# A threshold attention with a SwiGLU block: weight steps, x.T copies, key tails and q transposes moved between engines

## Chip, cores and metric

The kernel runs on one core of a Trainium2 chip. The metric is the device time of one execution in microseconds (us), the median of several runs. The profile is one execution recorded by the hardware profiler; its span is a little shorter than the device time.

## What is computed

Attention with a threshold for 8 batches, 8 heads, 576 positions and head size 64, and behind it a SwiGLU block over the 4608 tokens (model width 512, hidden width 1536). All is float32.

```python
scores = scale * np.matmul(q, k.transpose(0, 1, 3, 2))
thresh = np.max(scores, axis=-1, keepdims=True) - tau
scores = np.where(scores >= thresh, scores, -1000000000.0)
attn = np.exp(scores - np.max(scores, axis=-1, keepdims=True))
attn = attn / (np.sum(attn, axis=-1, keepdims=True) + 1e-09)
x = np.matmul(attn, v)              # (B,H,S,D) -> (B*S, H*D)
g = x @ w_gate
out = (g * (1.0 / (1.0 + np.exp(-g))) * (x @ w_val)) @ w_out
```

The weights come as float64 and are turned into float32 on the chip.

## The kernel before

**Order of work.** The schedule is written out by hand: each engine executes its instructions in the order in which the program issues them. The main loop goes over 36 segments. A segment is a pair of heads of one batch (`i`, 32 pairs, four to a batch) with a list of query tiles. The first four segments do tiles 0 and 1 of the first batch's pairs; the next four (segments 4 to 7, in the order of pairs 3, 0, 1, 2) do tiles 2, 3 and 4 of the same pairs; from segment 8 on a segment is a whole pair of a later batch with five tiles. A tile has 128 queries, and tile 4, the *short* tile, has the last 64. `TA = 2` tells the early tiles of the first batch from the late ones, `NT = 4` is the number of the short tile.

**One tile.** `scores` multiplies q and k on TensorE (PE; score banks `sc`), VectorE (DVE) takes the maximum (L328 in the first batch, L318 and L274 later), ScalarE (ACT) makes the threshold `th` (L333, later L330) and the exponential (L334), and VectorE masks and sums in one instruction (L338), which frees the score banks. The reciprocal `ri` follows; the normalisation (L352, L354) is shared between GpSimd (POOL) and ScalarE.

**First batch.** The probabilities have queries on the partitions. `flip` transposes them on PE one tile later: four blocks of 128 keys per head (`tp`, L396, or L398 where the normalisation is folded into the unit matrix, as in the early tiles), and the last 64 keys of each head by a product with the identity into the tile `end` (L400). ScalarE copies both to SBUF (L401, L406), and `attend_tile` multiplies with v (L421, L425); ScalarE copies the result into x.T (L427).

**Later batches.** The scores are laid out so that VectorE's own transposes of 32x32 blocks do the turning (L376). `attend` multiplies a whole pair with v (L447) in the second tile of the following pair, into two PSUM tiles `xa`, and then copies them into x.T: four copies of 128x128 (L458) and four of 64x32 (L466), alternately on VectorE and on ScalarE.

**q and k.** `prepare` transposes a pair's q and k on VectorE, one tile before the pair begins. In the first batch it does k (L758), the queries of the early tiles (L759), and the rest of q into a place of its own (L764; for pair 0 L763, one pair later).

**Weights.** 24 pieces pass through three steps, one piece further per tile: `fetch_weights` loads a piece (L182, L179), `split_weights` takes its high and low words apart on ScalarE (L193, L194), and `join_weights` puts them together: three instructions on VectorE (L202, L204, L205) and one on GpSimd (L207). In the main loop a tile's split stands ahead of its second half and its join behind the masking. What is not joined in time is done by `need`, ahead of the first product that uses it.

**SwiGLU.** Between the steps of a tile, `fill` issues gate and value products (`pg`, `pv`, L486) and output products (`po`, L554, L587), as many as `pace` allows. ScalarE takes the gate out of PSUM (`tn` L499, `gt` L500), VectorE multiplies with the value (L506), and GpSimd finishes the product (L518).

PSUM has two score tiles (`ps_s`, two banks each) and four banks for everything else (`ps_f`).

Of the kernel before, what the change touches and what calls it, by code (L numbers as in the profile page):

```python
# [19 lines left out]
def kernel(  # L20
# [30 lines left out]
    nc = tc.nc  # L51
# [224 lines left out]
    def same(out, in_):  # L276
        nc.scalar.copy(out, in_[:, :, 0])  # L277

    def scores(seg, t):
        qT, kT, tiles, halved = seg["qT"], seg["kT"], seg["tiles"], seg["halved"]  # L280
        if halved and "p" not in seg:
            seg["p"] = arenas[seg["i"] % 2]
        q0 = t * P - seg["q0"]
        heads = [slice(h * D, (h + 1) * D) for h in range(2)]
        if t < NT:
            pss = [ps_s.tile([P, 2, 512], F32, name="sc") for _ in range(2)]
            at = [t, NT + 1 + t]
        else:
            pss = [ps_s.tile([P, 2, 512], F32, name="sc")]
            at = [t]  # L290
        if halved:
            put = [(pss[u], h, q0 + u * D) for u in range(len(pss)) for h in range(2)]
            for x in range(0, len(put), 2):
                for g in range(NG):
                    a, c = divmod(g, 2)
                    for ps, h, col in put[x:x + 2]:
                        hs = heads[h]
                        nc.tensor.matmul(ps[g * G:(g + 1) * G, h, 0:SH], qT[hs, col + a * G:col + (a + 1) * G],  # L298
                                         kT[hs, c * SH:(c + 1) * SH], start=True, stop=True)
        elif t < NT:  # L300
            for h, hs in enumerate(heads):
                for n in range(2):
                    nc.tensor.matmul(pss[h][:, n, 0:SH], qT[hs, q0:q0 + P], kT[hs, n * SH:(n + 1) * SH],
                                     start=True, stop=True)
        else:
            for n, h in ((0, 0), (1, 1), (1, 0), (0, 1)):
                hs = heads[h]
                nc.tensor.matmul(pss[0][hs, n, 0:SH], qT[hs, q0:q0 + D], kT[hs, n * SH:(n + 1) * SH],
                                 start=True, stop=True)
        mx, nm, th, ri = (stp.tile([P, 4, 2] if x == "mx" else [P, 4], F32, name=x) for x in ("mx", "nm", "th", "ri"))  # L310
        sm = sums[0]
        sums.rotate(1)
        if halved:
            m = 2 * len(at)
            scs = [ps[:, h, 0:SH] for ps in pss for h in range(2)]
            ps = [seg["p"][:, x, u * SH:(u + 1) * SH] for u in range(2) for x in at]
            for x, tile_ in enumerate(pss):
                nc.vector.tensor_reduce(out=mx[:, 2 * x:2 * x + 2, 0], in_=tile_[:, :, 0:SH], axis=AX.X, op=ALU.max,  # L318
                                        negate=True)
            meet(mx, m, largest)  # L320
            nc.vector.tensor_reduce(out=nm[:, 0:m], in_=mx[:, 0:m, :], axis=AX.X, op=ALU.min)  # L321
        else:
            m = len(at)
            scs = [ps[:, :, 0:SH] for ps in pss]
            ps = [pbufs[0][:, x, :].rearrange("p (n s) -> p n s", n=2) for x in range(m)]
            pbufs.rotate(1)
            for x in range(m):
                nc.vector.tensor_reduce(out=nm[:, x:x + 1], in_=scs[x], axis=AX.XY, op=ALU.max, negate=True)  # L328
        if halved:
            nc.scalar.activation(th[:, 0:m], nm[:, 0:m], AF.Identity, bias=cut, scale=-1.0)  # L330
        for x in range(m):
            if not halved:
                nc.scalar.activation(th[:, x:x + 1], nm[:, x:x + 1], AF.Identity, bias=cut, scale=-1.0)  # L333
            nc.scalar.activation(ps[x], scs[x], AF.Exp, bias=nm[:, x:x + 1])  # L334
        yield
        turn(1)
        for x in range(m):
            nc.vector.scalar_tensor_tensor(out=ps[x], in0=scs[x], scalar=th[:, x:x + 1], in1=ps[x],  # L338
                                           op0=ALU.is_ge, op1=ALU.mult, accum_out=sm[:, x, 0:1])
        tot = stp.tile([P, 4], F32, name="tot")  # L340
        if halved:
            yield
            meet(sm, m, same)
            yield
            nc.vector.tensor_reduce(out=tot[:, 0:m], in_=sm[:, 0:m, :], axis=AX.X, op=ALU.add)
        else:
            nc.vector.tensor_reduce(out=tot[:, 0:m], in_=sm[:, 0:m, 0:3:2], axis=AX.X, op=ALU.add)
        nc.vector.reciprocal(out=ri[:, 0:m], in_=tot[:, 0:m])  # L348
        if t >= TA or halved:
            for x in range(m):  # L350
                if x % 2:
                    nc.gpsimd.tensor_scalar(out=ps[x], in0=ps[x], scalar1=ri[:, x:x + 1], scalar2=None, op0=ALU.mult)  # L352
                else:
                    nc.scalar.activation(ps[x], ps[x], AF.Copy, scale=ri[:, x:x + 1])  # L354
        if not halved:
            yield
        if halved:
            unturned.append([seg["p"][:, x, :] for x in at])
        else:
            units = [ident] * m  # L360
            if t < TA:

                units = [dbufs[0][:, x, :] for x in range(m)]
                dbufs.rotate(1)
                for x in range(m):
                    nc.scalar.activation(units[x], ident, AF.Copy, scale=ri[:, x:x + 1])
            unflipped.append((seg, t, [(p.rearrange("p n s -> p (n s)"), unit) for p, unit in zip(ps, units)]))
            yield
        yield

# [10 lines left out]
    def flip():  # L381

        if not unflipped:
            return
        seg, t, ps = unflipped.popleft()
        n = P if t < NT else D
        pT = pTbufs[0][:, 0:2 * KT * n].rearrange("p (h t q) -> p h t q", h=2, t=KT)
        pT2 = pTbufs[0][:, 2 * KT * n:(2 * KT + 1) * n]
        pTbufs.rotate(1)
        end = ps_f.tile([P, 512], F32, name="end", tag="psf")  # L390
        for h, (p, unit) in enumerate(ps):
            tp = ps_f.tile([P, 512], F32, name="tp", tag="psf")
            for kt in range(KT):
                ks = slice(kt * P, (kt + 1) * P)
                if unit is ident:
                    nc.tensor.transpose(tp[:, ks], p[:, ks], unit)  # L396
                else:
                    nc.tensor.matmul(tp[:, ks], p[:, ks], unit, start=True, stop=True)  # L398
            if t < NT:
                nc.tensor.matmul(end[h * D:(h + 1) * D, 0:P], p[:, KM:S], unit, start=True, stop=True)  # L400
                nc.scalar.copy(pT[:, h], tp.rearrange("p (t q) -> p t q", q=P))  # L401
            else:
                for hs in (slice(0, D), slice(D, P)):
                    nc.tensor.matmul(end[hs, 0:D], p[hs, KM:S], unit[hs, hs], start=True, stop=True)
                nc.scalar.copy(pT, tp.rearrange("p (t h q) -> p h t q", h=2, q=D))
        nc.scalar.copy(pT2, end[:, 0:n])  # L406
        unattended.append((seg, t, pT, pT2))
# [21 lines left out]
    def attend(seg):  # L429
# [21 lines left out]


        per = TC // (2 * G)
        puts = deque([nc.vector.tensor_copy, nc.scalar.copy])
        for a in range(R):
            for u in range(NU):
                i0 = 1 + u * per
                puts[0](xts["full", b * NU + u][:, cc, :, a, :],  # L458
                        xa[a][:, i0 * G:(i0 + per) * G].rearrange("d (i q) -> d i q", q=G))
                puts.rotate(1)  # L460
        at = b % BT
        for h in range(2):
            hs = slice(h * D, (h + 1) * D)
            cs = slice((1 + m) * G, (2 + m) * G) if h == 0 else slice(0, G)
            for a in range(2):
                puts[0](xts["last", b // BT][hs, cc, at, a], xa[a][hs, cs])  # L466
                puts.rotate(1)
        yield


# [267 lines left out]

    raws = {}
    kept = {}  # L740

    def fetch_qk(i):
        if i < NPAIR and i not in raws and i not in kept:
# [2 lines left out]
    def prepare(seg):  # L746
# [8 lines left out]
        if i < NP:  # L755
# [1 line left out]
            rest = flat[:, i * (S - QA):(i + 1) * (S - QA)]  # L757
            nc.vector.transpose(out=kT, in_=kr)  # L758
            nc.vector.transpose(out=qT[:, 0:QA], in_=qr[:, 0:QA])  # L759
            if i:  # L760
                if i == 1:

                    nc.vector.transpose(out=flat[:, 0:S - QA], in_=raws[0][0][:, QA:S])  # L763
                nc.vector.transpose(out=rest, in_=qr[:, QA:S])  # L764
            kept[i] = {"kT": kT, "qT": rest, "q0": QA}
        else:
            kT = qkp.tile([P, S], F32, name="kT")
# [17 lines left out]
    for n, seg in enumerate(segs):  # L785
        if NP <= n < 2 * NP:
            seg["v"] = segs[seg["i"]]["v"]
        for x, t in enumerate(seg["tiles"]):
# [28 lines left out]
            fill(part)  # L817
            next(go)
            gates()
            if attends and n > 2 * NP:  # L820
                next(products)
                next(products)
# [50 lines left out]
```

## Time and profile before

| | |
|---|---|
| time, median of 3 runs | 1536.05 us (1534.77 to 1539.76) |
| span of the profiled execution | 1532.6 us |
| PE busy | 1487.4 us (97%) |
| DVE busy | 1024.3 us (67%) |
| ACT busy | 729.7 us (48%) |
| POOL busy | 644.4 us (42%) |

Busy time of PE is modelled from pipelined matmuls, so a busy PE need not be at its peak. A mean share over the whole span mixes stages with different limits; the stages are read one by one below. Names such as `sc`, `pall` or `wgv` are tiles of the program, L338 is line 338 of the kernel, and an arrow in brackets names what ended an engine's wait.

### The profile page before, as it was taken

How to read it: one execution, taken by the hardware profiler on the slowest of the kernel's cores; microseconds unless marked ns; L12 is line 12 of the kernel's file. 1: busy time of each engine (PE TensorE's matmuls, PEld its weight loads, DVE VectorE, ACT ScalarE, POOL GpSimd, SP SyncE). 2: the span in 40 equal slices, each digit the busy share in tenths (PEclk: the TensorE clock that was granted, in tenths of full speed). 3: DMA queues.
4: the chain of work that ended last, by engine and by line, in shares of the span. 5: the costliest groups of instructions: out<-in, count | busy, mean ns of one | idle time of the engine just before them, and what ended most of it. 6: DMA issues, size and time to landing. Idle time of an engine off the chain costs nothing.

```text
span 1532.6 us, 31424 instructions
## 1 busy us (share of the span) xinstructions
PE 1487.4 (97%) x11792; PEld 1126.1 (73%) x11792; DVE 1024.3 (67%) x3150; ACT 729.7 (48%) x2045; POOL 644.4 (42%) x646
## 2 busy tenths in 40 slices
PE   6999889899999999999999999999999999999998
PEld 5766564477777777787777777777777777888887
DVE  6867988777777677756777777767776776522212
ACT  5777755555455545443454545544544454311110
POOL 3444544348354444435443545443535354400011
PEclk9999999999999999999999999999999999999999
DMA  8533312211111111110111111211101120000000
GB/s 199 137 104 125 87 30 53 50 39 32 27 29 41 29 32 46 46 32 14 36 29 46 32 46 32 46 32 41 26 27 31 46 47 15 1 14 1 14 15 14
DMA packets 176488, 66.93 MB, mean 44 GB/s; under 512 B 159696, under 2 KB 159696, under 8 KB 176336
## 3 DMA queue, kind: packets, MB, share of 16 engines
q1 hardware_dynamic: 168656, 54.88, 15.9%
q0 software_dynamic: 2944, 9.44, 1.7%
q8 instruction: 94, 1.54, 0.4%
q10 hardware_dynamic: 4736, 0.59, 0.3%
q14 instruction: 58, 0.48, 0.1%
HBM read 55.44 MB, written 9.44 MB: 42 GB/s over the span
## 4 chain that ended last, share of the span: by engine, by line
PE 85%; DVE 9%; ACT 2%; issue 1%; DMA 1%; SPq 1%; POOLq 0%; POOL 0%; DVEq 0%; ACTq 0%
PE pv L486 24%; PE pg L486 23%; PE po L587 19%; PE xa L447 8%; PE sc L298 8%; DVE pall L338 2%; DVE mx L318 2%; DVE pall L376 1%; DVE mx L274 1%; ACT pall L334 1%; DMA vall<-in_v_dram 1%; PE tp L396 1%; ACT sums L277 1%; SPq L242 0%; PE xa L421 0%
## 5 line engine op out<-in xcount | busy, mean ns | idle before, releaser
L352 POOL TENSOR_SCALAR pall<-pall,ri 128x288 f32<-128x288 f32 (+1 forms) x260 | 265.2, 1030 | 427.3 <-DVE ri L348 376.0
L486 PE MATMUL pg<-xall,wgv 128*128 128x256 f32 x1728 | 401.5, 384 | 1.3 <-ACT xall L427 1.3
L486 PE MATMUL pv<-xall,wgv 128*128 128x256 f32 x1728 | 401.6, 383 | 0.0
L486 PEld LDWEIGHTS pg<-xall,wgv 128*128 128x128 f32 x1728 | 324.4, 190 | 68.1 <-issue 17.9
L486 PEld LDWEIGHTS pv<-xall,wgv 128*128 128x128 f32 x1728 | 325.5, 191 | 64.4 <-issue 20.0
L338 DVE SCALAR_TENSOR_TENSOR pall<-sc,th,pall 128x288 f32<-128x288 f32 (+1 forms) x540 | 258.0, 528 | 24.3 <-ACT pall L334 24.3
L334 ACT ACTIVATE pall<-sc,nm 128x288 f32<-128x288 f32 (+1 forms) x540 | 236.3, 510 | 0.5
L318 DVE TENSOR_REDUCE mx<-sc 128x2 f32<-128x576 f32 x252 | 177.8, 742 | 31.3 <-PE sc L298 30.4
L354 ACT ACTIVATE pall<-pall,ri 128x288 f32<-128x288 f32 (+1 forms) x264 | 132.0, 540 | 104.8 <-DVE ri L348 103.5
L376 DVE STREAM_TRANSPOSE pall<-pall 128x576 f32<-128x576 f32 x252 | 181.3, 754 | 0.2 <-POOL pall L352 0.2
L298 PE MATMUL sc<-kT,qT 64*32 64x288 f32 x4032 | 158.6, 413 | 21.7 <-DVE pall L338 20.7
L587 PE MATMUL po<-wo,ht 128*128 128x256 f32 x768 | 176.2, 382 | 0.0
L506 DVE SCALAR_TENSOR_TENSOR ht<-tn,pv 128x512 f32<-128x512 f32 x102 | 69.8, 685 | 149.9 <-PE pv L486 147.1
L277 ACT COPY sums<-sums 32x4 f32<-32x4 f32 (+1 forms) x560 | 108.4, 194 | 124.0 <-DVE pall L338 112.7
L587 PEld LDWEIGHTS po<-wo,ht 128*128 128x128 f32 x768 | 144.4, 190 | 27.7 <-issue 4.6
L330 ACT ACTIVATE th<-nm,cut 128x4 f32<-128x4 f32 (+1 forms) x140 | 41.6, 297 | 231.8 <-DVE nm L321 231.8
L499 ACT ACTIVATE tn<-pg 128x512 f32<-128x512 f32 x108 | 64.9, 601 | 152.7 <-PE pg L486 152.0
L298 PEld LDWEIGHTS sc<-kT,qT 64*32 64x32 f32 x4032 | 59.1, 106 | 99.1 <-issue 71.4
L447 PE MATMUL xa<-pall,vall 64*64 64x288 f32 x2016 | 128.9, 405 | 0.6 <-issue 0.6
L518 POOL TENSOR_TENSOR ht<-ht,gt 128x512 f32<-128x512 f32 x84 | 106.6, 1271 | 33.3 <-ACT sums L277 21.4
L447 PEld LDWEIGHTS xa<-pall,vall 64*64 64x64 f32 x2016 | 77.5, 133 | 48.1 <-issue 5.3
L600 POOL TENSOR_TENSOR ht<-ht,xall 128x256 f32<-128x256 f32 x48 | 34.8, 728 | 179.5 <-PE po L587 177.2
(101 smaller groups left out, 1345.7 us busy)
## 6 DMA issues: line engine op xcount, KB each, us to landing
vall<-in_v_dram SPq DMA_DIRECT2D x112, 144.0 KB, 3.5
qraw<-in_q_dram SPq DMA_DIRECT2D x116, 72.0 KB, 2.4
kraw<-in_k_dram SPq DMA_DIRECT2D x116, 72.0 KB, 2.8
out_dram<-ob POOLq DMA_DIRECT2D x32, 256.0 KB, 2.4
wo<-in_moe_w_gate_dram SPq DMA_DIRECT2D x16, 384.0 KB, 3.5
wo<-in_moe_w_val_dram SPq DMA_DIRECT2D x16, 384.0 KB, 4.1
xall<-in_moe_w_out_dram SPq DMA_DIRECT2D x5, 768.0 KB, 4.7
wo<-in_moe_w_out_dram SPq DMA_DIRECT2D x3, 768.0 KB, 4.7
```

The costliest lines, as they stand in the source:

```text
L277: nc.scalar.copy(out, in_[:, :, 0])
L298: nc.tensor.matmul(ps[g * G:(g + 1) * G, h, 0:SH], qT[hs, col + a * G:col + (a + 1) * G], kT[hs, c * SH:(c + 1) * SH], start=True, stop=True)
L318: nc.vector.tensor_reduce(out=mx[:, 2 * x:2 * x + 2, 0], in_=tile_[:, :, 0:SH], axis=AX.X, op=ALU.max, negate=True)
L334: nc.scalar.activation(ps[x], scs[x], AF.Exp, bias=nm[:, x:x + 1])
L338: nc.vector.scalar_tensor_tensor(out=ps[x], in0=scs[x], scalar=th[:, x:x + 1], in1=ps[x], op0=ALU.is_ge, op1=ALU.mult, accum_out=sm[:, x, ...
L352: nc.gpsimd.tensor_scalar(out=ps[x], in0=ps[x], scalar1=ri[:, x:x + 1], scalar2=None, op0=ALU.mult)
L354: nc.scalar.activation(ps[x], ps[x], AF.Copy, scale=ri[:, x:x + 1])
L376: nc.vector.transpose(out=p, in_=p)
L447: nc.tensor.matmul(xa[a][h * D:(h + 1) * D, at:at + n * G].rearrange("d (i q) -> d i q", q=G), vr[rs, h, j, :], p[rs, lo:lo + n, j, :], st ...
L486: nc.tensor.matmul(ps[:, i], wgv[:, mat, c, (f + i) * P:(f + i + 1) * P], x[:, c, cs], start=(c == 0), stop=(c == NCC - 1))
L518: eng.tensor_tensor(out=hts[x], in0=hts[x], in1=gt, op=ALU.mult)
L587: nc.tensor.matmul(ps, h(f), w[:, f, :], start=(f == 0), stop=(f == NF2 - 1))
```

## The change

It has four parts, all of which move work between engines or in time.

1. *Last keys of both heads at once.* In the late tiles of the first batch (`turned`: tiles 2 and 3) head 1's keys are laid out rotated by 64, so that its last 64 keys stand first, right behind the last 64 keys of head 0. The two ends are then one block of 128 columns (`both`), and one transpose takes the place of two products with the identity. The rotated scores of head 1 need three products instead of two.
2. *Later q transposes.* The rest of q of pairs 1 and 2 is transposed in segment 4, behind its first two tiles, and no longer in the first two segments. It is needed in segments 6 and 7.
3. *Two weight steps in short tiles.* In the four short tiles of the first batch a second join, split and fetch is issued at the end of the tile.
4. *x.T copies.* All copies of `attend` are on ScalarE.

```diff
@@ scores
+                cut_ = D if turned(t) and h == 1 else 0
+                for n, lo, to in [(0, 0, D), (0, D, SH), (1, 0, SH)] if cut_ else [(0, 0, SH), (1, 0, SH)]:
+                    at_ = (n * SH + lo - cut_) % S
+                    nc.tensor.matmul(pss[h][:, n, lo:to], qT[hs, q0:q0 + P], kT[hs, at_:at_ + to - lo],
                                      start=True, stop=True)
...
+            both = pbufs[0].rearrange("p h s -> p (h s)")[:, KM:KM + P]
@@ flip
-                nc.tensor.matmul(end[h * D:(h + 1) * D, 0:P], p[:, KM:S], unit, start=True, stop=True)
+                if not turned(t):
+                    nc.tensor.matmul(end[h * D:(h + 1) * D, 0:P], p[:, KM:S], unit, start=True, stop=True)
+                elif h == 1:
+                    nc.tensor.transpose(end[:, 0:P], both, unit)
@@ attend
-        puts = deque([nc.vector.tensor_copy, nc.scalar.copy])
...
-                puts[0](xts["full", b * NU + u][:, cc, :, a, :],
-                        xa[a][:, i0 * G:(i0 + per) * G].rearrange("d (i q) -> d i q", q=G))
-                puts.rotate(1)
+                nc.scalar.copy(xts["full", b * NU + u][:, cc, :, a, :],
+                               xa[a][:, i0 * G:(i0 + per) * G].rearrange("d (i q) -> d i q", q=G))
...
-                puts[0](xts["last", b // BT][hs, cc, at, a], xa[a][hs, cs])
-                puts.rotate(1)
+                nc.scalar.copy(xts["last", b // BT][hs, cc, at, a], xa[a][hs, cs])
@@ prepare
-            if i:
-                if i == 1:
-
-                    nc.vector.transpose(out=flat[:, 0:S - QA], in_=raws[0][0][:, QA:S])
-                nc.vector.transpose(out=rest, in_=qr[:, QA:S])
+
+            later.append((rest, qr[:, QA:S]))
+            if i == 1 or i == NP - 1:
+                to, fr = later.pop(0 if i == 1 else -1)
+                nc.vector.transpose(out=to, in_=fr)
@@ main loop, behind gates()
+            if n == NP and later:
+                to, fr = later.pop(0)
+                nc.vector.transpose(out=to, in_=fr)
+            if t == NT and NP <= n < 2 * NP:
+
+                join_weights()
+                split_weights()
+                fetch_weights(2)
```

More of the change, by code (lines that the diff above doesn't have):

```diff
@@ L277, in same, with turned @@
         nc.scalar.copy(out, in_[:, :, 0])
+    def turned(t):
+        return TA <= t < NT
     def scores(seg, t):
@@ L301, in scores @@
             for h, hs in enumerate(heads):
-                for n in range(2):
-                    nc.tensor.matmul(pss[h][:, n, 0:SH], qT[hs, q0:q0 + P], kT[hs, n * SH:(n + 1) * SH],
+                cut_ = D if turned(t) and h == 1 else 0
+                for n, lo, to in [(0, 0, D), (0, D, SH), (1, 0, SH)] if cut_ else [(0, 0, SH), (1, 0, SH)]:
+                    at_ = (n * SH + lo - cut_) % S
+                    nc.tensor.matmul(pss[h][:, n, lo:to], qT[hs, q0:q0 + P], kT[hs, at_:at_ + to - lo],
                                      start=True, stop=True)
@@ L366, in scores @@
                     nc.scalar.activation(units[x], ident, AF.Copy, scale=ri[:, x:x + 1])
-            unflipped.append((seg, t, [(p.rearrange("p n s -> p (n s)"), unit) for p, unit in zip(ps, units)]))
+            unflipped.append((seg, t, both, [(p.rearrange("p n s -> p (n s)"), unit) for p, unit in zip(ps, units)]))
             yield
@@ L384, in flip @@
             return
-        seg, t, ps = unflipped.popleft()
+        seg, t, both, ps = unflipped.popleft()
         n = P if t < NT else D
@@ L393, in flip @@
             for kt in range(KT):
-                ks = slice(kt * P, (kt + 1) * P)
+                at = kt * P + (D if turned(t) and h == 1 else 0)
+                ks, to = slice(at, at + P), slice(kt * P, (kt + 1) * P)
                 if unit is ident:
-                    nc.tensor.transpose(tp[:, ks], p[:, ks], unit)
+                    nc.tensor.transpose(tp[:, to], p[:, ks], unit)
                 else:
-                    nc.tensor.matmul(tp[:, ks], p[:, ks], unit, start=True, stop=True)
+                    nc.tensor.matmul(tp[:, to], p[:, ks], unit, start=True, stop=True)
             if t < NT:
-                nc.tensor.matmul(end[h * D:(h + 1) * D, 0:P], p[:, KM:S], unit, start=True, stop=True)
+                if not turned(t):
+                    nc.tensor.matmul(end[h * D:(h + 1) * D, 0:P], p[:, KM:S], unit, start=True, stop=True)
+                elif h == 1:
+                    nc.tensor.transpose(end[:, 0:P], both, unit)
                 nc.scalar.copy(pT[:, h], tp.rearrange("p (t q) -> p t q", q=P))
@@ L740 @@
     kept = {}
+    later = []
     def fetch_qk(i):
```

## The prediction

> **What bounds the kernel now.** I read the windows by stage first, because the shares of the whole span average over stages with different limits. Stages: the first batch's short tiles beside the first gate products, 64 to 152 us; the second batch's first pair, 152 to 210; its other pairs, 210 to 305; the steady state, to 1310; the tail. Columns are busy time (and instructions) of PE, PEld, DVE, ACT, POOL, then granted clock, DMA share, GB/s.
>
> ```profile
> 64.00:152.00 88.00, 83.08 (x614) 59.61 (x612) 61.93 (x119) 63.23 (x123) 42.06 (x25) 1.00 0.33 104
> 152.00:210.00 58.00, 47.50 (x457) 34.04 (x449) 50.20 (x152) 38.39 (x100) 31.96 (x26) 0.94 0.32 76
> 210.00:305.00 95.00, 85.46 (x716) 45.97 (x708) 78.95 (x264) 51.27 (x156) 34.15 (x33) 0.98 0.22 47
> 305.00:1310.00 1005.00, 1002.67 (x8565) 760.16 (x8564) 724.21 (x2374) 500.50 (x1495) 482.11 (x503) 1.00 0.16 34
> ```
>
> See: from 305 us PE idles 2 us in 1005; 97% busy over the span hides about 40 us of PE idling, nearly all before 305. Next the chain of waits, stage by stage: from 305 it is PE alone to within 1%; from 152 to 305 it is mainly VectorE; from 64 to 152 it alternates. Its pieces (start, length, what) in the second stage:
>
> ```profile
> 173.68 0.47 ACT tn L499
> 174.15 0.48 ACT gt L500
> ...
> 175.91 1.32 DVE mx L318 x2
> 178.09 1.34 DVE pall L376 x2
> 179.43 1.72 DVE pall L338 x8
> 181.16 0.48 DVE wo L202
> 181.66 0.57 DVE wo L204
> 182.26 0.96 DVE wo L205
> 183.22 0.60 DVE ht L506
> ```
>
> L202, L204, L205 are a weight join: 2.0 us of VectorE inside the attention tile's chain. The timeline shows what that does to PE (the bracket is idle before, and who ended it):
>
> ```profile
> 196.68 0.72 PE L298 MATMUL sc<-kT,qT 64*32 64x288 f32 x16 [2.93 <-DVE pall L338]
> 197.56 0.72 PE L298 MATMUL sc<-kT,qT 64*32 64x288 f32 x16 [0.16 <-PE sc L298]
> 198.21 5.41 PE L486 MATMUL pv<-xall,wgv 128*128 128x256 f32 x16
> ```
>
> PE waits for VectorE to free the score banks, and then sixteen matmuls take 5.41 us; elsewhere they take 3.72.
>
> **What the Trainium skill says.** "TensorE: Matmul & The Clock Gate", What's actually happening: after an idle window of about 3.4 us the array runs at half clock until a busy one has passed. This trace agrees: clock 0.94 in that stage, and the 5.41. The same page, Terms: transpose mode is 4 times faster for FP32. Here a 128-column transpose is one instruction (four in 0.59 us, 0.15 each), and an `end` product with the identity, an ordinary fp32 matmul, is two instructions and 0.36 us on the chain. The same page, Architectural detail: ScalarE and VectorE are strict FIFO, so a waiting instruction holds all behind it. "SBUF — State Buffer", two separate sides: VectorE and GpSimd share a port pair under an exclusive lock. Here L204 takes 0.56 us, and 0.98 when a GpSimd L352 runs beside it.
>
> **The change part by part.**
>
> *Last keys of both heads at once (turned tiles, two of three per pair, eight in all).* Each removes two `end` products, 0.72 us, and adds one transpose, 0.15. The chain has both `end` pieces in five of these tiles (69.9, 77.95, 100.8, 123.2, 146.0) and one in three (93.7, 113.7, 138.9): 5 x 0.57 + 3 x 0.21 = 3.5 us. Against it, head 1's score block of 288 columns is split into 64 and 224: two more instructions a tile. Eight instructions of sc L303 take 1.18 us, 0.15 each, so at most 0.3 a tile; their columns don't grow, so at least 0.05. I take 0.2 on the five tiles whose sc is on the chain: +1.0. Net **-2.4** (-3.3 to -1.5).
>
> *Later q transposes.* L764 (0.39 us on the chain) leaves the first two pairs' tiles and comes back after two tiles of the next stage. The one at 28.5 is in a continuous VectorE chain: -0.4. The one at 15.4 lies beside cold PE and loads: half. There they return behind joins: before the next maximum VectorE idles 3.76 us after the first, and behind the second comes a short tile with 3.02 us idle: nothing. **-0.6** (-0.8 to -0.3).
>
> *Two weight steps in short tiles.* The instruction order of the two programs shows that the joins run between 173 and 203 us (four: three in the last tiles of the second batch's first pair, one in the tile of its attention product) go, one each, to the end of the four short tiles that start at about 75, 98, 120 and 143 us. What it removes I read from tiles of the next pair that have the same work but no join (from one maximum to the next): 175.91-167.89 = 8.02 against 216.63-209.95 = 6.68; 185.54-175.91 = 9.63 against 224.61-216.63 = 7.98; 192.16-185.54 = 6.62 against 229.56-224.61 = 4.95; then two tiles together 209.95-192.16 = 17.79 against 244.94-229.56 = 15.38, where the half clock goes too. 1.3 + 1.65 + 1.7 + 2.4 = **-7.0**. A join is 2.0, but 0.8 us of sums copies L277 on ScalarE, which it hid, shows again. PE has room: 47.5 busy of 58, 3.5 of it clock loss.
>
> What it costs where it goes: VectorE gets 2.1 us more per short tile. Behind the join waits the next tile's maximum L328. After the first two short tiles VectorE idles 3.0 us there: hidden. In the third the order puts the join behind L506, which waits for PE:
>
> ```profile
> 125.38 0.96 DVE L205 SCALAR_TENSOR_TENSOR wgv<-wo,wgv 128x768 uint32<-128x768 uint32 x1
> 128.19 0.69 DVE L506 SCALAR_TENSOR_TENSOR extra<-tn,pv 128x512 f32<-128x512 f32 x1 [1.85 <-PE pv L486]
> 129.35 1.42 DVE L328 TENSOR_REDUCE nm<-sc 128x1 f32<-128x576 f32 x2 [0.47 <-PE sc L303]
> ```
>
> so the 1.85 us can't be used, 2.1 less 0.47 is exposed, and that chain runs on to 138: +1.7. In the fourth, likewise behind L506 (149.29), the join ends about 152.1 for a maximum at 151.73: +0.35. ScalarE: the extra split (L193, L194, 1.95 us) stands after tn and gt, which wait for pg, and ahead of the next th L333. In the first short tile gt ends 84.04, so th starts near 86.0 instead of 84.91: +1.0. In the second gt ends 105.85 and th is due at 107.74: nothing; in the others ScalarE is free. The last weight load can be issued only after the fourth extra join, about 152, and its median landing is 4.7 us; its split now starts at 156.5 and would wait half a microsecond: +0.5. GpSimd's part (1.81 each) fits beside its 42 busy of 88. Sum **+3.5** (+1 to +8, the latter if each join and split is exposed whole). Net -3.5.
>
> *x.T copies.* Per pair VectorE loses two copies of 128x128 and two of 64x32, 0.9 us; ScalarE then does eight in about 1.8 us. In the second batch's pairs:
>
> ```profile
> 279.02 0.30 DVE xall L458
> 279.35 0.28 ACT xall L458
> 279.65 0.18 DVE xall L466
> 279.84 0.20 DVE xall L466
> 280.07 1.43 DVE mx L318 x2
> ```
>
> The maximum begins 1.05 us after the attention product ends. Without copies it waits only for the first half of the scores, which PE issues behind that product (16 instructions, about 0.65). Saved 0.4 on four pairs: **-1.6** (-2.5 to 0). ScalarE's next work, th, comes some 2.4 us after its copies now, which takes 0.9 more. In the 24 later pairs PE is the chain, the next products use other PSUM banks first, and 0.9 us less VectorE work buys nothing.
>
> Sum: -2.4 - 0.6 - 7.0 + 3.5 - 1.6 = -8.1; 1536.05 - 8.1 = **1528.0 us**.
>
> **The rivals.**
> - *More is won (1521):* the moved steps hide nearly whole (+0.5), another half-clock spell goes (-1.8), the other terms come at their far ends (-3.3, -0.8, -2.5): -15. For it: 26 us of VectorE idle in the first batch. Against: strict order behind L506.
> - *The joins only change place (1531.5):* exposed as much as they save, C nil: -4.6. For it: the chain from 84 to 93 and 128 to 138 is VectorE and ScalarE already.
> - *PE takes over in the second batch (1533.5):* with output products a tile is 5.42 + 1.20 = 6.6 us of PE against 6.7 of VectorE, so of the 7.0 only 3 arrive and the copies bring nothing: -2.4 - 0.6 - 3 + 3.5 = -2.5. Against: PE idles 10.5 us from 152 to 210.
> - *Slower (1541):* joins and splits exposed whole with late loads (+8.2 + 2 - 7), and the longer copies make PE wait 0.2 in 24 pairs (+4.8), less 3 for the first two parts: +5. For it: ScalarE is strict FIFO, and carries 63 of 88 us in the first batch before. Against: slack of 2 us and more ahead of most th.
>
> **How the numbers follow.** Chances: forecast 0.61, more 0.12, change of place 0.13, PE takes over 0.08, slower 0.06. Faster by over 0.3% is below 1531.4: forecast, more, and half of the change of place, 0.80; slower 0.06; the rest 0.14. The range goes from the 1521 of the larger gain to 1534, past PE taking over.
>
> **What would show it.** Right: 152 to 210 us has no join after its second tile, shrinks by some 7 us and its clock nears 1.00; `end` is a single instruction; the next maximum after an attention product starts about 0.7 us after it; from 305 on the PE chain has its old length. Wrong: th L340 behind the extra split in more than one tile, PE waiting for ScalarE's xall copies in the steady state, or the stage from 64 to 152 growing by over 3 us.

## The result and the profile after

The changed kernel takes 1531.44 us (median of six runs, 1530.09 to 1533.89), the kernel before 1537.1 us (six runs, 1534.77 to 1539.76) beside it. The ratio is 0.9965, with a 95% interval of [0.9952, 0.9977]: faster by a third of a per cent. The span of the profiled execution went from 1532.6 to 1528.3 us.

The windows of the changed kernel, by the same stages as before (columns: busy time and instructions of PE, PEld, DVE, ACT, POOL; granted clock, DMA share, GB/s):

```profile
64.00:152.00 88.00, 79.32 (x570) 60.74 (x567) 71.50 (x128) 67.07 (x128) 45.51 (x26) 0.98 0.38 117
152.00:210.00 58.00, 49.25 (x495) 33.60 (x494) 48.89 (x148) 34.55 (x100) 30.02 (x24) 0.97 0.26 56
210.00:305.00 95.00, 84.67 (x721) 43.87 (x720) 76.75 (x253) 53.86 (x170) 34.81 (x34) 1.00 0.22 47
305.00:1310.00 1005.00, 1003.06 (x8570) 762.11 (x8569) 706.03 (x2287) 512.68 (x1592) 485.55 (x506) 1.00 0.16 34
```

VectorE has 9.6 us more in the first stage. Three of the four extra joins lie in it, 6.2 us of plain work, and the two q transposes that moved there, 1.0 us; so a good part of the rest is time in which an instruction runs and doesn't get on. PE has 3.8 us less there: the turned ends take less, and the stage takes longer, so that its end falls out of the window. The steady state is as it was. Where the time went, I read from the start of the maximum of 17 tiles, named segment x tile (5x0 is the first tile of segment 5). First column: the kernel before, in us. Then the difference of each kernel to it; the four single parts and the change without its first part are explained below.

```
tile  before   ends   steps  copies  q tr.  no ends  AFTER
4x0    59.33  +0.29  +0.62   -0.05  +0.64   +0.71   +0.05
4x2    76.10  +0.36  +0.61   -0.05  +1.07   +1.14   +0.55
5x0    84.12  -0.82  +1.05   -0.05  +0.64   +1.56   +0.97
5x2    98.85  -1.76  +3.06   -0.05  +2.29   +3.36   +0.19
6x0   106.94  -2.72  +3.52   -0.05  +2.30   +3.82   +0.66
6x2   121.26  -2.72  +3.51   -0.05  +2.30   +3.82   +2.28
7x0   129.35  -3.68  +5.97   -0.04  +2.31   +6.28   +4.10
7x2   144.09  -4.63  +7.64   -0.05  +3.99   +6.26   +3.15
8x0   151.73  -5.59  +9.93   -0.05  +4.00   +8.55   +5.43
8x1   159.63  -5.53  +9.86   +0.19  +3.99   +8.59   +5.35
8x4   185.47  -5.52  +6.68   +0.19  +4.03   +5.41   +2.16
9x2   209.95  -5.54  +2.61   -0.06  +4.05   +1.01   -2.24
10x2  244.94  -5.54  +2.73   -0.39  +4.07   +0.83   -2.44
12x1  306.20  -5.58  +2.69   -0.29  +4.15   +0.59   -2.57
12x2  317.99  -6.76  +1.51   -0.52  +4.62   -0.91   -4.07
24x0  813.08  -6.77  +1.87   -0.84  +4.63   -1.23   -4.38
35x4 1318.82  -6.77  +1.87   -0.84  +4.62   -1.23   -4.38
```

Read the last column as a story: the first batch ends 5.4 us *later* than before, the second batch's first pair wins 7.6 (from 8x1 to 9x2), and behind 305 us only 1.8 more come, nearly all in one step. One caution: a step of some 1.2 to 1.8 us can be a spell of PE at half clock (3.4 us long in these traces), and these spells sit at other places in other profiles. The step at 12x2 is one of them: the kernel before had such a spell at 304 us, and four of the six columns step down there likewise. A table of one execution each is good for places; for sizes under 2 us the ratios decide. Some 0.6 us of offset can stand at 4x0 though nothing ahead of it was edited, as in the steps' column.

The second batch, in the chain of waits of the changed kernel (start, length, what), where the kernel before had a join at 181.16:

```profile
176.75 1.74 DVE pall L345 x8
...
178.51 0.20 ACT sums L277
...
179.39 0.18 DVE tot L352
...
179.59 0.18 DVE ri L355
179.77 1.32 DVE mx L324 x2
```

Masking, sums, reciprocal, next maximum: no join stands between them, and the sums copies on ScalarE that it used to hide are seen, 0.8 us as reckoned. The x.T copies of a pair of that batch, in the timeline of the changed kernel (start, length, engine, line, operation):

```profile
276.63 0.74 ACT L468 COPY xall<-xa 128x128 f32<-128x128 f32 x4
277.25 0.55 ACT L475 COPY xall<-xa 64x32 f32<-64x32 f32 x4
277.48 1.42 DVE L324 TENSOR_REDUCE mx<-sc 128x2 f32<-128x576 f32 x2 [1.94 <-PE sc L301]
```

All eight copies take 1.2 us on ScalarE (reckoned: 1.8), the maximum waits for PE's scores alone and starts 0.75 us after the attention product.

Now the first batch. The timeline of the changed kernel at the end of the first short tile, at an idle time of PE in segment 6, and at the end of the fourth short tile:

```profile
81.54 0.55 DVE L202 TENSOR_SCALAR wgv<-wgv 128x768 f32<-128x768 f32 x1
81.77 2.00 POOL L207 TENSOR_TENSOR wgv<-wgv,extra 128x768 uint32<-128x768 uint32 x1 [2.87 <-DVE wgv L205]
82.13 2.05 DVE L204 TENSOR_SCALAR wgv<-wgv 128x768 uint32<-128x768 uint32 x1
84.22 0.96 DVE L205 SCALAR_TENSOR_TENSOR wgv<-wo,wgv 128x768 uint32<-128x768 uint32 x1
85.09 1.42 DVE L335 TENSOR_REDUCE nm<-sc 128x1 f32<-128x576 f32 x2
...
117.03 5.35 PE L494 MATMUL pg<-xall,wgv 128*128 128x256 f32 x16 [2.21 <-ACT xall L438]
...
152.45 1.83 POOL L207 TENSOR_TENSOR wo<-wo,extra 128x768 uint32<-128x768 uint32 x1 [4.57 <-DVE wo L205]
152.83 1.87 DVE L202 TENSOR_SCALAR wo<-wo 128x768 f32<-128x768 f32 x1
154.24 1.60 POOL L526 TENSOR_TENSOR extra<-extra,gt 128x512 f32<-128x512 f32 x1
154.73 1.52 DVE L204 TENSOR_SCALAR wo<-wo 128x768 uint32<-128x768 uint32 x1
```

The extra join isn't a second copy of the first. L204, which takes 0.56 us elsewhere, takes 2.05 where GpSimd's addition L207 of the *first* join of the same tile started 0.36 us ahead of it, and it ends at 84.18, 0.41 us after that addition (spans on GpSimd are rough in the profile). So most of its work, which takes 0.56 us alone, is done behind the addition. At 152.83 it is L202, 1.87 in place of 0.55, and L204 again behind the next GpSimd instruction. From start to next instruction the extra joins take 3.55, 3.56, 3.34 and 4.34 us in the four short tiles, not 2.1. At 117.03 sixteen matmuls take 5.35 us in place of 3.72, behind 2.21 us of idle PE.

### The profile page after: what moved, and what is told of

Read it like the earlier page. It is cut to its first block, busy times and chain, and to the rows that moved or that the text cites. A ratio compares the mean times of both kernels' runs of the same rounds, so it can differ in the third digit from the quotient of the medians.

```text
span 1528.3 us, 31412 instructions
## 1 busy us (share of the span) xinstructions
PE 1480.7 (97%) x11784; PEld 1123.4 (74%) x11784; DVE 1006.4 (66%) x3038; ACT 742.8 (49%) x2157; POOL 645.7 (42%) x646
## 4 chain that ended last, share of the span: by engine, by line
PE 83%; DVE 12%; ACT 3%; issue 1%; DMA 1%; SPq 0%; DVEq 0%; POOLq 0%; POOL 0%; ACTq 0%
PE pv L494 23%; PE pg L494 23%; PE po L595 19%; PE sc L301 8%; PE xa L458 8%; DVE pall L345 3%; DVE mx L324 2%; DVE pall L383 2%; ACT pall L341 1%; DVE mx L274 1%; ACT sums L277 1%; DVE nm L335 1%; DVE wgv L205 1%; DVE wgv L204 1%; PE sc L309 1%
## 5 line engine op out<-in xcount | busy, mean ns | idle before, releaser
L526 POOL TENSOR_TENSOR ht<-ht,gt 128x512 f32<-128x512 f32 x84 | 106.7, 1272 | 33.2 <-DVE tot L352 21.9
```

Source lines behind the costliest of these rows:

```text
L526: eng.tensor_tensor(out=hts[x], in0=hts[x], in1=gt, op=ALU.mult)
```

## The experiments

The theories after the result: (1) the ends work as the prediction has it; (2) the extra joins cost more than they save unless GpSimd's additions are kept from them (the lock); (3) the q transposes and the copies are small. The rivals: the ends gain nothing, because PE has idle time in that stage, and all of the gain is the weight steps; or the parts need each other. Each kernel was timed in five rounds beside the kernel before.

**Each part alone.** Four kernels, each the kernel before with one part of the diff shown above: the ends (hunks `scores`, `flip`), the steps (the last `if` of the main loop), the copies (hunk `attend`), the q transposes (hunk `prepare` and the `pop` behind `gates()`).

> Only the turned tiles (last keys of both heads transposed at once); everything else as before. Theory of the prediction: -2.4 us, because five tiles have both end products on the chain. Rival: the first batch's tiles end on VectorE's chain, so the PE time saved turns into a longer PE wait, and PE may even drop to half clock after it: between -1 and +1 us at the start of the second batch.

> Only the extra weight steps in the four short tiles; everything else as before. Theory of the prediction: the joins leave the second batch (-7.0 us) and cost 3.5 us in the first: -3.5. Theory of the port lock, formed from the changed kernel's trace: the extra join costs 3.3 to 4.3 us instead of 2.0, because its L202 and L204 wait for a GpSimd instruction that is under way (L207 of the join before, or the gates), so the first batch grows by about 5 us and the whole gains 2 to 3.

> Only the x.T copies, all on ScalarE. Theory of the prediction: 0.4 us in each of the second batch's four pairs, -1.6, and nothing in the later ones. Rival: later pairs lose by ScalarE's longer copies, 0 or above.

> Only the later q transposes. Theory of the prediction: -0.6 us. Rival, from the changed kernel's trace: the 0.3 us won in the first segment is lost again at the next wait, and the transpose behind the second tile of segment 4 pushes the short tile's maximum back by 0.4: between -0.1 and +0.4.

| part alone | median, us | ratio | interval |
|---|---|---|---|
| ends | 1530.29 | 0.9959 | [0.9944, 0.9974] |
| weight steps | 1536.17 | 1.0001 | [0.9991, 1.0010] |
| x.T copies | 1536.90 | 0.9996 | [0.9987, 1.0005] |
| q transposes | 1538.91 | 1.0006 | [0.9998, 1.0014] |

The ends alone give all that the change gives, more than either number on record for them (-2.4, or -1 to +1). That the weight steps were the gain falls: alone they are nothing to a thousandth, where the prediction had -3.5 and the lock theory -2 to -3, because in the table they lose 9.9 us up to 8x0 (some 3.4 of it two half-clock spells, at 5x2 and 7x2) and win 7.2 from 8x1 to 9x2. The copies are told neither from nothing nor from the -1.6 of the prediction: their interval runs from -2.0 to +0.8 us. The q transposes are not told from nothing either, but a gain of 0.6 us lies outside their interval. Of the 4 us in their column 3.3 are two half-clock spells (5x2, 7x2) and the rest stood at 4x0 already.

Why the ends pay 0.95 us a tile and not 0.57 is in the chain of waits. The kernel before, in the tile at 99 us:

```profile
99.83 0.36 PE xa L425 x4
100.19 0.59 PE tp L396 x4
100.78 0.36 PE end L400 x2
101.14 0.59 PE tp L396 x4
101.73 0.36 PE end L400 x2
102.09 1.93 PE pg L486 x8
```

and the ends alone, in the same tile:

```profile
98.06 0.37 PE xa L436 x4
98.43 1.02 PE tp L404 x8
99.45 0.11 PE end L411
99.56 1.73 PE pg L497 x8
```

The two `end` products go from 0.72 to 0.11 (-0.61; I had -0.57). But eight transposes in one go take 1.02 where two groups of four took 1.18 (-0.16), and the eight gate matmuls behind them take 1.73 where they took 1.93 (-0.20). Sum -0.97, and the table shows it at six places of the ends' column (-1.18 at 5x0, then five times -0.94 to -0.96). In these tiles, an ordinary float32 product set between transposes thus costs more than its own length: the instructions around it take longer too. Why they do, no run here shows.

**The change without the ends.** All of the change but the first part:

> The changed kernel without the turned tiles. If the turned tiles bring what the prediction said, it is 2.4 us slower than the changed kernel. If the first batch is bound by VectorE once the extra joins are there, it is within 1 us of it, and the sixteen gate products that took 5.35 us at 117 us in the changed kernel take about 3.7 again, as PE idles less before them.

Measured 1534.47 us, ratio 0.9990 [0.9978, 1.0001]. So within the change the ends are worth 2 to 4 us, less than alone: 0.0025 of the ratio, 3.0 by the medians, and 2.5 from 4x0 to the last tile (-4.43 against -1.94). The sixteen gate products that took 5.35 us at 117 us take 3.72 again, behind 1.46 us of idle PE, as expected; but a half-clock spell stands at 95 us instead. The table says where the rest of the gain went. From 4x2 to 5x0 the ends alone win 1.2 us, but the change loses 0.42 with the ends and 0.42 without: the extra join has made VectorE the chain in that tile, and what PE saves is no longer on it. At 6x0 it is the same (+0.47 with, +0.46 without), and at 8x0 (+2.28, +2.29). The ends still pay at 5x2, at 7x2 and partly at 7x0.

**Is it the lock?** Three kernels change the order of the joins and additions, or do without two of them. In the first, the addition of the first join stands behind VectorE's part of the second in the program. In the second, both joins of a short tile stand in the place of the first, with both additions behind them. (In these two, `join_weights` issues VectorE's part of its pieces first; its changed body is not shown.) In the third, only the first two short tiles have extra steps.

```diff
@@ e6_add_late, behind the masking
-                join_weights()
+                held = join_weights(-1 if short else 1)
...
@@ e6_add_late, at the end of a short tile
-                join_weights()
+                join_weights(1, held)
@@ e7_both_early, behind the masking
-                join_weights()
+                join_weights(2 if t == NT and NP <= n < 2 * NP else 1)
...
@@ e7_both_early, at the end of a short tile
-                join_weights()
@@ e8_two_short
-            if t == NT and NP <= n < 2 * NP:
+            if t == NT and NP <= n < NP + 2:
```

> The changed kernel, with the GpSimd add of a short tile's first join issued only behind the VectorE part of its second join, at the tile's end. Nothing is left out. Port lock: in the first two short tiles the second L204 falls from 2.06 us to about 0.56, in the last the second L202 from 1.87 to about 0.55; the start of the second batch moves 1.5 to 3 us forward. Rival (the cost is the strict order on ScalarE or VectorE alone): the durations stay, and so does the time.

> The changed kernel, with both joins of a short tile one behind the other in the middle of the tile, ahead of L506 (here L516), and both GpSimd adds behind them; the extra split and load stay at the end. Nothing is left out. If the cost of the extra joins is the port lock and the place behind L506, a join takes 2.0 us, fits in VectorE's idle time, and about 4 us of the 5 lost in the first batch come back: some 4 us below the changed kernel. If it is the extra split on ScalarE, the time stays.

> The changed kernel, with extra weight steps in the first two short tiles only, so that two of the four joins go back to the second batch. By the changed kernel's trace the last two extra joins cost 1.8 and 2.3 us, and the two joins that come back cost 1.7 and 2.4: about the same time, within 1 us.

Measured: 1534.41 us, 0.9986 [0.9980, 0.9993]; 1532.09 us, 0.9971 [0.9961, 0.9982]; 1531.35 us, 0.9967 [0.9956, 0.9978]. The first two are misses, and not because the lock theory fell: the edits didn't take the lock away. The timeline of the second of them (the first has the same 2.06 us in its first two short tiles):

```profile
82.22 2.00 POOL L209 TENSOR_TENSOR wgv<-wgv,extra 128x768 uint32<-128x768 uint32 x1 [2.87 <-DVE wgv L205]
82.58 2.06 DVE L204 TENSOR_SCALAR wgv<-wgv 128x768 uint32<-128x768 uint32 x1
```

GpSimd is idle and starts the addition as soon as the first piece's L205 is done, wherever the program writes it: order in the text holds an engine only against its own earlier instructions. That the first comes out some 3 us slower than the change goes with the half clock: its 22 executions show a granted clock of 0.992 to 0.994, those of the change 0.994 to 0.997. Leaving out two of the four extra joins (the third kernel) changes nothing either, as it would if a join costs in its short tile about what it saves later.

**The lock, taken away.** So, with both joins in the place of the first as before, the two additions were issued in the other order, the second piece's first (`los.rotate(1)` gives the next split the buffer that is freed first). GpSimd works through its instructions in order, and the second piece isn't ready until VectorE is through with both. One kernel has this in the whole change; one has it without the q transposes; and a third has only the ends and the copies, to see what the change is worth without its second and third part.

```diff
@@ join_weights, two pieces in a short tile
-        for up, place, ub, lb in ups:
+        if len(ups) == 2:
+            los.rotate(1)
+        for up, place, ub, lb in reversed(ups):
             nc.gpsimd.tensor_tensor(out=ub, in0=ub, in1=lb, op=ALU.add)
```

> Parts 1 and 4 of the change alone (the turned ends, the x.T copies on ScalarE); the weight steps and the q transposes are as before. If the parts add (ends alone 0.9959, copies alone 0.9996, steps and transposes nothing or a small loss), the ratio is about 0.9955, some 2 us faster than the whole change, and the first batch ends about 5.5 us earlier than before with no loss behind it. The rival, that the parts help each other (the steps need the room that the ends give), expects no better than the whole change: 0.9965 or above.

> The whole change, with the two joins of a short tile one right behind the other on VectorE, and GpSimd's two additions issued in the other order: the one for the second piece first. GpSimd takes its work in order, so no addition can start before VectorE is through with both pieces, and none runs beside L204. The lock theory expects L204 at 0.56 us in the second join in place of 2.06, and 1.5 us less in each short tile whose join is exposed: about 1529 to 1530, a ratio of 0.9950 to 0.9960 (the same two joins with additions in the old order: 0.9971). If the room isn't on the chain, or if the wait comes back at the split, whose buffer an addition frees 2 us later, the ratio stays at 0.9965 to 0.9975.

> As the run before it, but without part 2 (q transposes where they were before): the ends, the copies and the two joins of a short tile with GpSimd's additions in the other order. If the q transposes bring nothing, as alone, it is equal to the run before it within 0.001; if they cost where the change puts them (behind the first tiles of segment 4), it is about 0.0005 lower. If the lock theory holds, it is at or below the ends and copies alone (0.9955).

| kernel | median, us | ratio | interval |
|---|---|---|---|
| ends and copies | 1527.55 | 0.9941 | [0.9926, 0.9957] |
| the change, additions turned | 1529.66 | 0.9952 | [0.9933, 0.9970] |
| the same without q transposes | 1530.53 | 0.9960 | [0.9944, 0.9976] |

The timeline of the second of them, in the first short tile and the tile behind it:

```profile
82.53 0.55 DVE L202 TENSOR_SCALAR wgv<-wgv 128x768 f32<-128x768 f32 x1
83.12 0.56 DVE L204 TENSOR_SCALAR wgv<-wgv 128x768 uint32<-128x768 uint32 x1
83.72 0.96 DVE L205 SCALAR_TENSOR_TENSOR wgv<-wo,wgv 128x768 uint32<-128x768 uint32 x1
...
84.82 3.59 POOL L211 TENSOR_TENSOR wgv<-wgv,extra 128x768 uint32<-128x768 uint32 x2 [4.92 <-DVE wgv L205]
...
86.67 1.01 ACT L194 ACTIVATE extra<-wo,minus 128x768 f32<-128x768 uint32 x1 [1.49 <-POOL wgv L211]
87.59 0.28 ACT L345 ACTIVATE th<-nm,cut 128x1 f32<-128x1 f32 x1
...
88.53 0.82 DVE L350 SCALAR_TENSOR_TENSOR pall<-sc,th,pall 128x576 f32<-128x576 f32 x1 [2.52 <-ACT pall L346]
```

L204 is back at 0.56 us, the whole second join at 2.06, as the lock theory says. The ratio, 0.9952, lies where that theory had it, but it isn't told from the whole change (0.9965), and the 1.5 us can't be found in the trace: the additions now end later, the extra split's L194 waits 1.49 us for the buffer it frees, `th` stands behind L194 on ScalarE, and the masking waits 2.52 us for ScalarE where it would wait 0.33. A wait on VectorE had become a wait on ScalarE. The kernel without q transposes is level with it within a thousandth, as expected, and it comes out above the ends and copies alone (0.9960 against 0.9941, with intervals that overlap a little), where the lock theory had it level or below. Nor do the parts need each other: without the weight steps the kernel comes out at least as fast.

**The split moved, too.** The last kernel is the one without q transposes, with the extra split moved into the next tile, behind `th` and the exponential.

```diff
@@ main loop, short tile
-                split_weights()
@@ main loop, where a tile splits
                 split_weights()
+                if x == 0 and NP < n <= 2 * NP:
+                    more = 1
+                    split_weights()
```

> The run e11_ends_turned with one thing moved: the extra split of each short tile stands in the next tile, behind its th and its exponential and beside the split that is there anyway. VectorE's order is the same instruction by instruction. In the short tile that split waited for a buffer that GpSimd's addition frees (L194 idle 1.5 to 2.7 us), and th, behind it on ScalarE, waited with it, so VectorE's masking idled about 2.4 us in three tiles. If that wait is where the gain of the turned additions went, th starts within 1 us of its maximum in these tiles, the first batch ends 3 to 5 us earlier than in e11_ends_turned (0.996), and the ratio falls to about 0.992 to 0.994, level with or below the ends and copies alone (0.9941). If the wait only moves on to the next tile's join, the ratio stays at 0.995 to 0.997.

Measured 1530.62 us, 0.9958 [0.9945, 0.9971]: the number of the second expectation, by which the wait moves on. Its timeline:

```profile
84.17 0.29 ACT L345 ACTIVATE th<-nm,cut 128x1 f32<-128x1 f32 x1 [1.00 <-DVE nm L340]
...
87.32 1.73 POOL L364 TENSOR_SCALAR pall<-pall,ri 128x576 f32<-128x576 f32 x1
87.50 0.98 DVE L202 TENSOR_SCALAR wgv<-wgv 128x768 f32<-128x768 f32 x1 [0.35 <-ACT wgv L193]
88.51 0.95 DVE L204 TENSOR_SCALAR wgv<-wgv 128x768 uint32<-128x768 uint32 x1
```

`th` is prompt (0.79 us after its maximum). But now the next tile's join has its split only just ahead of it, starts 0.35 us late and beside GpSimd's normalisation L364, and takes 0.98 and 0.95 where it takes 0.54 and 0.56 alone.

Another part of what is missing is half clock. Two stretches of PE in this kernel, and below them the same two in the kernel that it was made from:

```profile
93.48 3.46 PE L499 MATMUL pv<-xall,wgv 128*128 128x256 f32 x8
117.24 5.33 PE L499 MATMUL pg<-xall,wgv 128*128 128x256 f32 x16 [1.68 <-ACT xall L443]
...
95.92 1.89 PE L499 MATMUL pv<-xall,wgv 128*128 128x256 f32 x8
119.35 3.72 PE L499 MATMUL pg<-xall,wgv 128*128 128x256 f32 x16 [2.21 <-ACT xall L443]
```

The first batch ends 1.3 us earlier than there, with 3.2 us lost in these two spells; without them it would be 4.5 (an estimate from these lines), within the 3 to 5 of the first expectation. So its mechanism came, and the spells took most of it. All six executions show a low granted clock, 0.992 to 0.995, where the kernel that it was made from has 0.996 and 0.997. Whether this edit brings the spells isn't shown.

At 8x0 the three orders (the change, additions turned, split moved) stand at +5.43, +4.56 and +3.42 us against the kernel before, and the ends with copies at -3.35: four more joins and splits cost 7 to 9 us up to there in every order, half-clock spells included (one in each first batch, and three where the split moved), and win some 7 behind it.

The best version measured is the ends with the copies: 0.9941, against 0.9965 for the whole change. The intervals overlap by a hair ([0.9926, 0.9957] and [0.9952, 0.9977]), so it is likely the better kernel, by 3.7 us in the ratios and 1.2 at the last tile of one profile each, and not certainly. How much of it is the copies isn't settled: with the ends alone the ratio was 0.9959, the two intervals overlap widely, and at the last tile of one profile each the ends with copies stand at -5.6 us against -6.8 for the ends alone, with one half-clock spell of 1.7 us in the first batch that the other doesn't have.

How much of each gain is half clock can be seen by comparing executions with the same granted clock. At 0.997 the means are 1534.1 us for the kernel before (9 of its 106 in these experiments), 1531.1 for the change (4 executions), 1533.2 without the ends (5), 1528.5 for the ends alone (3) and 1526.9 for the ends and copies (4). By these few, the change is worth 3.0 us at an equal clock, the ends 5.6 alone and 2.1 inside it, and the ends with copies 7.2. The ends' gain is therefore not made of spells, and some half of the change's is.

## Why the prediction was right, and where it wasn't

1531.44 us lies in the range, and the forecast of faster holds. The gain is 5.7 us of the 8.1 expected, and its parts are not those of the sum. At an equal granted clock it is 3.0, as seen above. The rest is fewer half-clock spells than in the kernel before, of which the sum counted one; whether the change brings this or chance isn't shown, so that the total came as near as it did is in part luck.

- **Last keys: -2.4, measured about -6 alone and -2 to -4 inside the change.** The mechanism was right, the size too small. Each step of the ends is 0.97 us and not 0.57: I took the transposes and the gate product around the `end` products as unchanged, and they lose 0.16 and 0.20. It happens at six tiles, where I had five and three smaller ones. And the +1.0 for the split score block was too much: in the ends' column no tile behind such a block loses time; in the chain of the changed kernel nine of its instructions take 1.29 us against 1.18 for eight, 0.11.
- **q transposes: -0.6, measured nothing** (1.0006, at best -0.0002). The step that failed is the gain in the first stage. In the q transposes' own profile the maximum at 15.8 us starts 0.4 earlier against the tile ahead of it, but the next one waits 2.43 us for PE's scores, and in the kernel before it waits for them too, 1.29: it was not VectorE that held it. The maximum at 28.9 us does gain 0.7 against its tile ahead, 0.4 of it the transpose that is gone, but in the next join L202 takes 0.96 in place of 0.54, beside a GpSimd instruction that it didn't meet before, and 0.4 is gone again. Where the transposes come back, 4x2 starts 0.43 us later in two columns (alone and without the ends), and alone that is made good by 5x0, as I had it.
- **Weight steps, won in the second batch: -7.0, measured -7.2 alone and -7.6 in the change.** Reading tiles with the same work but no join as the price of a join was right to within the reading. One half-clock spell in that stage goes with it, as the sum had it, and the granted clock rises from 0.94 to 0.97, though not to 1.00.
- **Weight steps, cost in the first batch: +3.5, measured +5.0 at its four places, about 9 against the ends and copies, with the gain of the ends that it swallows.** The places are +0.42 (5x0), +0.47 (6x0), +1.82 (7x0) and +2.28 (8x0). The third was reckoned at 1.7, and that it came out so is luck: the join itself was 3.34 us, not 2.1, and the ends gave part of it back (+2.46 without them). The fourth was reckoned at 0.35, and that is the step that failed. I counted the plain 2.1 us; the lock adds 1.32 to L202 and 0.96 to L204. I had named the lock, with L204 at 0.98 beside a GpSimd instruction, and then didn't put the two additions of one tile beside the second join. My +1.0 for `th` behind the extra split failed too: in the first short tile the split ends at 85.1, within VectorE's longer join, and `th` (85.88) waits for its maximum, not for the split. The +0.5 for the late load didn't come either: the last split, at 161.99, starts right behind a copy. The sign that I had named for a failure, the stage from 64 to 152 growing by over 3 us, came: 5.4.
- **A half-clock spell of +1.6 us at 117.03** stands in the changed kernel's first batch and was in no term. PE's idle ahead of it is 2.21 us; the kernel before has 1.34 there and full speed behind it. But the changed kernel itself idles 2.23 us at 94.1 and runs at full speed behind that, and the kernel with the split moved has half clock behind 1.35 and 1.68. "TensorE: Matmul & The Clock Gate" in the Trainium skill (What's actually happening) has idleness lead to half clock, which would make it the work of the extra joins, for they bring VectorE and so ScalarE's copy late. The page's idle window is about 3.4 us, longer than any of these, so the length of one idle time doesn't tell. That isn't settled: of the profiles with extra steps each has one to three such spells in the first batch, of those without them three have none, one has one and one has two.
- **x.T copies: -1.6, measured -0.6** (0.9996, interval -2.0 to +0.8), and -0.8 at the last tile of their profile. The mechanism was right: the maximum behind an attention product starts 0.2 to 0.3 us earlier, in the second batch (9x2, 10x2, 11x2) and in nearly every later pair. The size failed, 0.4 on each of four pairs: the gain is mostly given back within the pair, that of 10x2 at 10x4, where the column stands at -0.04 again.

The rival "the joins only change place" (1531.5) describes the weight steps best, and its number is the measured one. But it got there with the small figure for the ends; the ends carried the gain and the steps ate part of it.

## What to carry to other kernels

Don't move work into idle time of one engine without looking at its neighbours in that time: a moved VectorE instruction cost up to 3.7 times its length because GpSimd had an instruction of the step before it running. A delay that is removed only by making another instruction later comes back behind that instruction, so follow what is queued behind it before the edit. Before a slower version is given up, compare executions at an equal granted clock: the kernel with the split moved lost over 3 us to half clock that its edit may or may not have caused. And where the tensor engine is the chain, count the changes between transposes and ordinary products, not only the instructions: a part that looked like 0.57 us a tile was 0.97, and dropping the cleverer parts of a change gave what is likely the better kernel.

## What the hardware showed that I had not expected

- **The lock's size.** "SBUF — State Buffer" in the Trainium skill (two separate sides) says that GpSimd, and VectorE in those of its instructions that use the shared ports, hold them one at a time, for a whole instruction. This case agrees: a join's L204 took 0.56 us alone, 0.98 beside a normalisation (L352 in the kernel before), 1.5 beside a product L526, and 2.05 when the addition L207 had just begun. GpSimd's addition went from 1.81 to 2.00 in the last case. The reduction L335 out of PSUM, which ran beside the other additions, stayed at 1.42 for two. When the additions were kept away, the second join's L204 was 0.56 in all four short tiles.
- **Switching between transposes and float32 products.** Four transposes, a product of two instructions, and the same again took 1.90 us, and eight gate matmuls behind them 1.93; eight transposes and one more took 1.13, and the eight behind them 1.73. 0.36 us of the 0.97 is outside the removed instructions.
- **Half-clock spells vary from execution to execution** of one kernel: the granted clock of the kernel before went from 0.991 to 0.997 over its 106 executions in the experiments, and its mean time from 1540.0 us at the one to 1534.1 at the other. A spell was worth up to 1.7 us, so two single profiles can differ by 2 us and more for nothing that was edited.
